# Attention's products placed on tiles of the TensorE array: two heads on two partition halves

## The chip, the cores and the metric

One core of one Trainium2 chip runs the whole program in one launch. The metric is the device time of an execution in microseconds (us). TensorE is called PE here, VectorE DVE, ScalarE ACT, GpSimd POOL, and SyncE, which issues most DMAs, SP. PEld is PE's loading of weights, which the profile lists apart from its matmuls.

## The reference

A linear attention with a decaying state (batch B = 4, heads H = 8, sequence S = 768, head dimension D = 48) is followed by a mixture of experts with one expert per token (N = 3072 tokens, width 384, E = 8 experts, inner width F = 1024). All arrays are 32-bit floats.

```
for t in range(S):                       # attention, per batch and head
    cur = einsum('bhd,bhe->bhde', u * k_t, v_t)
    y_t = einsum('bhd,bhde->bhe', r_t, state + cur)
    state = w * state + einsum('bhd,bhe->bhde', k_t, v_t)
x = y as (N, 384)
e_idx = argmax(x @ w_gate, axis=1)       # top-1 routing
gate_w = softmax(x @ w_gate)[token, e_idx]
eom = sigmoid(x @ w_output_gate)
out[token] = gate_w * eom[token, e] * (relu(x @ w1[e]) @ w2[e])   # e = e_idx
```

## The kernel before, in words

Attention is done in chunks of C = 128 tokens: 6 chunks per batch, 24 in all. Inside a chunk r and k are multiplied by powers of w (tables `PR` and `PK`), so that the decay between two tokens becomes a product. The loop `for i in range(NT)` in `rwkv_top1_moe` walks the chunks, and for each it walks the list `STEP` (`STEP0` for chunk 0), in which each short name is a piece of work handed out by `act`. The whole stretch is in manual order: each engine runs its instructions as the program writes them.

The pieces of a chunk, by their names in `STEP`:

- `s0`, `s1` (`scores`): q = 0..3 is a pair of heads, j the head in the pair. A transposed K of a pair has 96 partitions (2 x 48). `KT` holds it twice, each copy with the other head's rows set to zero (a scale by `k.block`), so a 96-row matmul gives one head's 128 x 128 scores. DVE multiplies them by the causal mask into `A[j]` (L281).
- `st` (`state`): K^T V for a pair, 96 x 96 with two unwanted off-diagonal blocks, which the decay `WT` sets to zero. DVE adds the old state (L302), POOL multiplies by `WT` (L303).
- `in` (`inter`): r times the old state, 4 matmuls into the bank `ps_y`.
- `i0`, `i1` (`intra`): masked scores times v, 8 matmuls into the same bank.
- `tr` (`trans`): the next chunk's K and R are transposed on PE (L266) and copied by ACT, K twice (L271), R once (L268).
- `xt`, `lm`, `lt`: the finished chunk's output x is transposed (L363), copied by ACT, multiplied by the router's two weights into 16 logits (L370), which ACT copies out a chunk later.
- `p0`, `p1` (`prep`, L213), `ut` (`uterm`, POOL) and `bo` (`bonus`): r and k times the powers, and the term with u. `ld` loads chunk i + 3. After the list, `output` adds the u-term to `ps_y` (L325) and stores x.
- `m` (`micro`), `t1`, `t5`: small steps of the router's grouping program, some on DVE, some on PE.

All these matmuls are in 32-bit floats; the profile shows each as two records of a weight load and a matmul, and each transpose as one. The experts behind attention use fp32r matmuls, with one record each. The first expert's first rows are gathered and multiplied while the last chunk and the last router group are finished.

Of the kernel before, what the change touches and what calls it, by code (L numbers as in the profile page):

```python
# [41 lines left out]
HW = 2 * D  # L42
# [5 lines left out]
STEP = ['lt', 's0', 'm', 's1', 'm', 'xt', 'ld', 'ut', 'bo', 'm', 'p0', 'm', 'p1', 'st', 'm', 'in', 'tr', 't5', 'm', 'i0', 'i1', 'lm', 't1']  # L48
# [83 lines left out]
def make_flag(tc, pool, pspool, k):  # L132
    nc = tc.nc
    ok = pool.tile([HW, NP], F32, name="ok")
# [3 lines left out]
    nc.tensor.matmul(ps[:, :NP], k.ones[:HW], ok, start=True, stop=True)  # L138
    return ps


def read_flag(tc, pool, ps, k):
# [4 lines left out]
    nc.vector.tensor_scalar(k.flag, low, float(HW) - 0.5, None, op0=ALU.is_ge)  # L147


def make_powers(tc, pool, k, halfway):  # L150
    nc = tc.nc
    M = C // 2
    sq = [pool.tile([HW, NP], F32, name=f"sq{i}") for i in range(8)]
    pr = pool.tile([HW, NP, C], F32, name="pr_t")
# [1238 lines left out]
```

## Time and profile before

| | us |
|---|---|
| median of 3 runs | 433.81 (431.82 to 435.5) |
| profiled execution | 432.96 |
| its span | 431.2 |
| first scores of chunk 0 | start at 8.23 |
| scores of chunk 23, the last | start at 170.85 |
| PE busy | 405.2 (94%) |
| DVE busy | 259.4 (60%) |
| ACT busy | 170.5 (40%) |
| POOL busy | 175.7 (41%) |

The profiled execution took 1.76 us more than its span, from the first to the last instruction. A page of the profile counts an engine as busy from an instruction's start to its end; PE's ends are modelled, and neighbouring matmuls overlap, so a block's price on PE is read from start to start. Bracketed times in an order of time are the idle time before an instruction, with what ended it. In the groups, the columns are busy time, mean nanoseconds of one, and idle time ahead with its releasers. The granted clock of PE is 0.979 of full speed as a mean over the span, and 1.00 in attention from 0 to 160 us.

### The profile page before, as it was taken

What the parts mean: (1) busy time and instruction counts of PE and PEld (TensorE: products, weight loads), DVE (VectorE), ACT (ScalarE), POOL (GpSimd) and SP (SyncE); (2) the same over time, 40 slices, a digit from 0 to 9 for tenths busy, and PEclk for the clock granted to TensorE, in tenths of its full rate; (3) what the DMA queues carried; (4) which work ended last, traced back from release to release, by engine and by line L of the source; (5) the groups of instructions that cost most, each with busy time, mean ns of one, the idle gap of its engine ahead of it and who ended that gap; (6) DMA issues with size and microseconds to landing.
All of it is one profiled execution on the core that took longest, in us unless ns stands there. A gap on an engine that the chain in (4) does not pass through costs nothing. (4 is left out here: it accounts for less than half of the span.)

```text
span 431.2 us, 8139 instructions
## 1 busy us (share of the span) xinstructions
PE 405.2 (94%) x2948; PEld 396.6 (92%) x2948; DVE 259.4 (60%) x592; ACT 170.5 (40%) x339; POOL 175.7 (41%) x210
## 2 busy tenths in 40 slices
PE   7899999999999989995998999999999999999980
PEld 5899999999999989995997999999999999999980
DVE  6966698597769996381676356166274653636300
ACT  4323333342425344421545255265363552535210
POOL 6965446646456779523115031132212502301020
PEclk9999999999999999898899999999999999999996
DMA  7855646464557753006427336365274472840010
GB/s 138 175 114 109 136 87 147 95 129 109 111 112 181 204 137 121 21 19 218 138 85 245 111 117 198 96 194 169 58 241 148 132 233 75 258 127 34 2 42 20
DMA packets 104669, 54.83 MB, mean 127 GB/s; under 512 B 78495, under 2 KB 102227, under 8 KB 104608
## 3 DMA queue, kind: packets, MB, share of 16 engines
q1 hardware_dynamic: 101184, 44.27, 39.7%
q0 software_dynamic: 3424, 9.82, 6.9%
q8 instruction: 29, 0.48, 0.5%
q14 instruction: 32, 0.26, 0.2%
HBM read 44.64 MB, written 9.76 MB: 126 GB/s over the span
## 5 line engine op out<-in xcount | busy, mean ns | idle before, releaser
L835 POOL DMA_INDIRECT out_dram<-yo,si x28 | 28.5, 1018 | 135.5 <-ACT yo L832 72.8
L798 PE MATMUL ps_h<-xh,w1h 128*128 128x384 f32 (+4 forms) x216 | 74.0, 343 | 6.5 <-issue 4.7
L799 PE MATMUL ps_h<-xl,w1h 128*128 128x384 f32 (+4 forms) x216 | 72.2, 334 | 0.0
L800 PE MATMUL ps_h<-xh,w1l 128*128 128x384 f32 (+4 forms) x216 | 72.1, 334 | 0.0
L769 POOL DMA_INDIRECT xg<-x_d,gi x28 | 31.5, 1125 | 44.6 <-PE ps_xt L781 29.8
L798 PEld LDWEIGHTS ps_h<-xh,w1h 128*128 128x128 f32 x216 | 42.3, 196 | 7.6 <-issue 5.0
L279 PE MATMUL ps_a<-RT,KT 96*128 96x128 f32 x384 | 48.6, 280 | 0.4 <-DVE RT L231 0.4
L808 DVE SCALAR_TENSOR_TENSOR hl<-ps_h,hh 128x384 fp32r<-128x384 f32 (+4 forms) x72 | 37.8, 532 | 17.4 <-ACT hh L807 17.1
L807 ACT ACTIVATE hh<-ps_h 128x384 fp32r<-128x384 f32 (+4 forms) x72 | 33.6, 472 | 33.0 <-PE ps_h L800 33.0
L279 PEld LDWEIGHTS ps_a<-RT,KT 96*128 96x128 f32 x384 | 44.8, 192 | 0.8 <-DVE RT L231 0.8
L860 PE MATMUL ps_o<-w2h,hh 128*128 128x384 f32 x128 | 43.5, 340 | 0.0
L861 PE MATMUL ps_o<-w2l,hh 128*128 128x384 f32 x128 | 42.9, 335 | 0.0
L862 PE MATMUL ps_o<-w2h,hl 128*128 128x384 f32 x128 | 42.8, 335 | 0.0
L281 DVE TENSOR_TENSOR A<-ps_a,mask 128x512 f32<-128x512 f32 x48 | 32.6, 684 | 16.6 <-PE ps_a L279 16.5
L800 PEld LDWEIGHTS ps_h<-xh,w1l 128*128 128x128 f32 x216 | 42.3, 196 | 0.2
L799 PEld LDWEIGHTS ps_h<-xl,w1h 128*128 128x128 f32 x216 | 42.3, 196 | 0.1
L747 DVE TENSOR_TENSOR w1l<-raw,w1h 128x768 fp32r<-128x768 f32 x28 | 26.7, 954 | 23.4 <-ACT w1h L746 23.4
L271 ACT ACTIVATE KT<-ps_t,block 96x512 f32<-96x512 f32 x46 | 28.9, 678 | 27.9 <-PE ps_t L266 27.9
L319 PE MATMUL ps_y<-v_t,A 128*128 128x48 f32 x336 | 39.7, 271 | 0.0
L319 PEld LDWEIGHTS ps_y<-v_t,A 128*128 128x128 f32 x336 | 39.2, 192 | 0.0
L746 ACT CAST w1h<-raw 128x768 fp32r<-128x768 f32 (+1 forms) x36 | 27.2, 764 | 27.0 <-PE ps_h L799 17.4
L253 POOL TENSOR_TENSOR vc<-v_t,coef 128x384 f32<-128x384 f32 x21 | 21.9, 1044 | 38.0 <-DVE coef L251 27.5
(222 smaller groups left out, 808.6 us busy)
## 6 DMA issues: line engine op xcount, KB each, us to landing
raw<-in_moe_w_dram SPq DMA_DIRECT2D x64, 384.0 KB, 4.9
x_d<-x SPq DMA_DIRECT2D x24, 192.0 KB, 2.0
k_t<-in_k_dram SPq DMA_DIRECT2D x21, 192.0 KB
r_t<-in_r_dram SPq DMA_DIRECT2D x21, 192.0 KB, 4.8
v_t<-in_v_dram SPq DMA_DIRECT2D x21, 192.0 KB, 4.7
raw<-in_k_dram SPq DMA_DIRECT2D x3, 192.0 KB
raw<-in_r_dram SPq DMA_DIRECT2D x3, 192.0 KB
xg<-x_d,gi POOLq DMA_INDIRECT x28, 4.8
```

The lines of the kernel that those rows point to most:

```text
L279: nc.tensor.matmul(pa[:, q, :], KT[:, q, j, :], RT[:, q, :], start=True, stop=True)
L281: nc.vector.tensor_mul(a, pa, k.mask.unsqueeze(1).to_broadcast((C, NP, C)))
L319: nc.tensor.matmul(self.y[:, D * h : D * (h + 1)], A[j][:, h // 2, :], vt[:, h, :], start=(i % NCH == 0 and h == 0), stop=(h == H - 1), sk ...
L769: nc.gpsimd.indirect_dma_start(out=self.xg[q][:n], out_offset=None, in_=self.x_d[:n_x, :], in_offset=bass.IndirectOffsetOnAxis(ap=self.rt. ...
L798: nc.tensor.matmul(o, wh[:, j, fs], xh, start=(j == 0), stop=False)
L799: nc.tensor.matmul(o, wh[:, j, fs], xl, start=False, stop=False)
L800: nc.tensor.matmul(o, wl[:, j, fs], xh, start=False, stop=(j == KC - 1))
L807: nc.scalar.activation(hh, o, AF.Relu)
L808: nc.vector.scalar_tensor_tensor(hl, o, 0.0, hh, op0=ALU.max, op1=ALU.subtract)
L860: nc.tensor.matmul(o, hh, wh, start=(f == 0), stop=False)
L861: nc.tensor.matmul(o, hh, wl, start=False, stop=False)
L862: nc.tensor.matmul(o, hl, wh, start=False, stop=(f == FC - 1))
```

## The change: what it does

Head j of a pair now lives on partitions 64 j to 64 j + 47, with zeros in the 16 partitions above. `Rn` and `Kn` become fixed tiles with 64 columns per head, whose last 16 columns are set to zero once. The tables, the powers and the state follow that layout, and `k.block`, `WT` and K's second copy are gone. Each product is then written for a part of the array:

- scores: for each head 48 rows (its half of the partitions) and, in two column halves c, 64 of the 128 keys: 16 matmuls in place of 8, in tiles of 64 x 64. The two heads' products are interleaved, and the two masks (`a0`, `a1`) follow the whole block (`sc`).
- inter: the same quarters, 16 matmuls in place of 4. `ps_y` has two banks, one for each head j.
- intra, state and logits: all 128 rows, 64 columns: 16, 8 and 6 matmuls in place of 8, 4 and 3, in tiles of 128 x 64.

The state is 128 x 192 in place of 96 x 384, without the off-diagonal blocks. `xt` takes its PSUM bank from the two score banks (`at`), and the logits take theirs from the state's (`u`); logits are multiplied and copied out in one step, `lm`, a chunk earlier. `STEP` is written in another order, the loading of w comes in two DMAs behind a memset on DVE, and k and r of chunk 0 are loaded into tiles padded in the same way.

PE in one chunk before (chunk 3; `ps_a` are scores, `ps_x` transposes of the output and then logits, `ps_u` the state, `ps_y` inter and intra, `ps_t` transposes of the next chunk):

```order
L279 MATMUL ps_a_576<-RT,KT 128x128 x4
L279 MATMUL ps_a_583<-RT,KT 128x128 x4
L363 MATMUL ps_x<-ident,x 128x128 x3
L295 MATMUL ps_u<-v_t,Kn 96x96 x4
L312 MATMUL ps_y<-T,RT 128x96 x4
L266 MATMUL ps_t<-ident,Kn 96x128 x4
L266 MATMUL ps_t<-ident,Rn 96x128 x4
L319 MATMUL ps_y<-v_t,A_581 128x48 x4
L319 MATMUL ps_y<-v_t,A_588 128x48 x4
L370 MATMUL ps_x<-wg_149,xT 128x16 x3
```

PE in one chunk after (chunk 4; only the last two of eight rows of scores are shown, and `ps_l` are the logits):

```order
L277 MATMUL ps_a_771<-RT,KT 64x128 x2
L277 MATMUL ps_a_772<-RT,KT 64x128 x2
L315 MATMUL ps_y<-T,RT 64x48 x16
L372 MATMUL ps_x<-ident,x 128x128 x3
L264 MATMUL ps_t<-ident,Kn_301 128x128 x4
L264 MATMUL ps_t<-ident,Rn_298 128x128 x4
L382 MATMUL ps_l<-wg_151,xT 64x16 x6
L323 MATMUL ps_y<-v_t,A_789 64x48 x8
L293 MATMUL ps_u<-v_t,Kn_300 64x48 x8
L323 MATMUL ps_y<-v_t,A_791 64x48 x8
```

Inter has moved up behind the scores, the state from in front of the transposes to between the two halves of intra, and the logits from the end to in front of intra. Scores and inter stand side by side, and so do all products in column halves.

DVE in one chunk without router steps before (masks, u-term's sum, R and K times their powers, the state's add, the output):

```order
L281 TENSOR_TENSOR A_1209<-ps_a_1204,mask 128x512
L281 TENSOR_TENSOR A_1216<-ps_a_1211,mask 128x512
L251 TENSOR_REDUCE coef<-ku 128x8
L213 TENSOR_TENSOR Rn<-r_t,PR 128x384
L213 TENSOR_TENSOR Kn<-k_t,PK 128x384
L302 TENSOR_TENSOR T_1247<-ps_u,T 96x384
L325 TENSOR_TENSOR x<-ps_y,vc 128x384
```

DVE in such a chunk after:

```order
L281 TENSOR_TENSOR A_1404<-ps_a_1386,mask 128x512
L281 TENSOR_TENSOR A_1406<-ps_a_1387,mask 128x512
L249 TENSOR_REDUCE coef<-ku 128x8
L217 TENSOR_TENSOR Rn_298<-r_t,PR 128x8x48
L217 TENSOR_TENSOR Kn_301<-k_t,PK 128x8x48
L301 TENSOR_TENSOR T_1486<-ps_u,T 128x192
L330 TENSOR_TENSOR x<-ps_y,vc 128x384
```

The order on DVE is the same; the state's add has half the columns, and R and K are written with a step of 64 per head.

The diff, cut to its core:

```
-STEP = ['lt', 's0', 'm', 's1', 'm', 'xt', 'ld', 'ut', 'bo', 'm', 'p0', 'm', 'p1', 'st', 'm', 'in', 'tr', 't5', 'm', 'i0', 'i1', 'lm', 't1']
+STEP = ['m', 'sc', 'a0', 'm', 'a1', 'in', 'xt', 't1', 'm', 'tr', 't1', 'ld', 'ut', 'bo', 'm', 'p0', 'm', 'p1', 'lm', 'i0', 'st', 'i1', 'm']
...
-    k.wt = pool.tile([HW, NP], F32, name="wt")
-    tc.nc.sync.dma_start(k.wt, w.rearrange("(q j) d -> (j d) q", j=2))
+    k.wt = pool.tile([C, NP], F32, name="wt")
+    tc.nc.vector.memset(k.wt, 1.0)
+    for j in range(2):
+        tc.nc.sync.dma_start(k.wt[HB * j : HB * j + D], w.rearrange("(q j) d -> j d q", j=2)[j])
...
+        self.Rn, self.Kn = ([self.pw.tile([C, H, HB], F32, name=f"{nm}{i}", bufs=1) for i in range(n)] for nm, n in (("Rn", 2), ("Kn", 3)))
+        for t in self.Rn + self.Kn:
+            tc.nc.gpsimd.memset(t[:, :, D:], 0.0)
...
-            if src is Rn:
-                nc.scalar.copy(RT, p[:HW])
-            else:
-                for j in range(2):
-                    nc.scalar.activation(KT[:, :, j, :], p[:HW], AF.Copy, scale=k.block[:, j, 0:1])
+            nc.scalar.copy(dst, p)
...
-        pa = ps.tile([C, NP, C], F32, name=f"ps_a{j}", tag="at", bufs=2)
+        self.pa = [ps.tile([C, NP, C], F32, name=f"ps_a{j}", tag="at", bufs=2) for j in range(2)]
         for q in range(NP):
-            nc.tensor.matmul(pa[:, q, :], KT[:, q, j, :], RT[:, q, :], start=True, stop=True)
+            for j in range(2):
+                rows = slice(HB * j, HB * j + D)
+                for c in range(2):
+                    half = slice(HB * c, HB * (c + 1))
+                    nc.tensor.matmul(self.pa[j][half, q, :], KT[rows, q, half], RT[rows, q, :], start=True, stop=True)
...
-        for q in range(NP):
-            nc.tensor.matmul(U[:HW, HW * q : HW * (q + 1)], Kf[:, HW * q : HW * (q + 1)], vt[:, 2 * q : 2 * q + 2, :], start=True, stop=True)
+        for h in range(H):
+            j, q = h % 2, h // 2
+            nc.tensor.matmul(U[HB * j : HB * (j + 1), D * q : D * (q + 1)], Kn[:, h, :], vt[:, h, :], start=True, stop=True)
...
-                nc.tensor.matmul(self.y[:, HW * q : HW * (q + 1)], RT[:, q, :], self.T[:, q, :], start=(q == 0), stop=False, skip_group_check=True)
+                for j in range(2):
+                    rows = slice(HB * j, HB * j + D)
+                    for c in range(2):
+                        half = slice(HB * c, HB * (c + 1))
+                        nc.tensor.matmul(self.y[half, j, D * q : D * (q + 1)], RT[rows, q, half], self.T[rows, q, :], start=(q == 0), stop=False, skip_group_check=True)
...
-        for h in range(j, H, 2):
-            nc.tensor.matmul(self.y[:, D * h : D * (h + 1)], A[j][:, h // 2, :], vt[:, h, :], start=(i % NCH == 0 and h == 0), stop=(h == H - 1), skip_group_check=True)
+        for q in range(NP):
+            for c in range(2):
+                half = slice(HB * c, HB * (c + 1))
+                nc.tensor.matmul(self.y[half, j, D * q : D * (q + 1)], A[j][:, q, half], vt[:, 2 * q + j, :], start=(i % NCH == 0 and q == 0), stop=(q == NP - 1), skip_group_check=True)
...
-        px = ps.tile([C, 512], F32, name="ps_x", tag=tag, bufs=1)
+        px = ps.tile([C, 512], F32, name="ps_x", tag=tag, bufs=bufs)
...
+        pl = ps.tile([C, 512], F32, name="ps_l", tag=tag, bufs=1)
         for j in range(KC):
-            self.tc.nc.tensor.matmul(px[:, DM : DM + 2 * E], xT[:, j, :], self.wg32[:, j, :], start=(j == 0), stop=(j == KC - 1), skip_group_check=True)
+            for c in range(2):
+                half = slice(HB * c, HB * (c + 1))
+                self.tc.nc.tensor.matmul(pl[half, : 2 * E], xT[:, j, half], self.wg32[:, j, :], start=(j == 0), stop=(j == KC - 1), skip_group_check=True)
...
-                                X[i - 1] = rt.logits_t(ps, rw, x)
+                                X[i - 1] = rt.logits_t(ps, rw, x, "at", 2)
```

More of the change, by code (lines that the diff above doesn't have):

```diff
@@ L41 @@
 EARLY = 2
-HW = 2 * D
+HB = 64
 ORDER_AT = 14
@@ L137, in make_flag @@
     ps = pspool.tile([C, 512], F32, name="ps_flag", tag="g", bufs=1)
-    nc.tensor.matmul(ps[:, :NP], k.ones[:HW], ok, start=True, stop=True)
+    nc.tensor.matmul(ps[:, :NP], k.ones, ok, start=True, stop=True)
     return ps
@@ L152, in make_powers @@
     M = C // 2
-    sq = [pool.tile([HW, NP], F32, name=f"sq{i}") for i in range(8)]
-    pr = pool.tile([HW, NP, C], F32, name="pr_t")
-    pk = pool.tile([HW, NP, C], F32, name="pk_t")
+    sq = [pool.tile([C, NP], F32, name=f"sq{i}") for i in range(8)]
+    pr = pool.tile([C, NP, C], F32, name="pr_t")
+    pk = pool.tile([C, NP, C], F32, name="pk_t")
     nc.vector.memset(pr[:, :, M : M + 1], 1.0)
@@ L178, in make_tables, with load_rkv @@
     for src, dst in ((k.pk, k.PK), (k.pr, k.PR)):
-        ps = pspool.tile([C, NP, HW], F32, name="ps_pw", tag="tr", bufs=2)
+        ps = pspool.tile([C, H, HB], F32, name="ps_pw", tag="tr", bufs=2)
         for q in range(NP):
-            nc.tensor.transpose(ps[:, q, :], src[:, q, :], k.ident[:HW, :HW])
-        nc.scalar.copy(dst.rearrange("p h d -> p (h d)"), ps.rearrange("p q d -> p (q d)"))
-    for q in range(NP):
-        nc.scalar.activation(k.WT[:, q, :], k.block.rearrange("p j d -> p (j d)"), AF.Copy, scale=k.w128[:, q : q + 1])
-def load_rkv(tc, pin, spare, srcs, b, c, after=None):
+            nc.tensor.transpose(ps[:, 2 * q : 2 * q + 2, :], src[:, q, :], k.ident)
+        nc.scalar.copy(dst, ps[:, :, :D])
+def load_rkv(tc, pin, spare, srcs, b, c, first, after=None):
     nc = tc.nc
@@ L217, in first @@
         nc, k = self.tc.nc, self.k
-        RT = self.pw.tile([HW, NP, C], F32, name="RT")
-        KT = self.pw.tile([HW, NP, 2, C], F32, name="KT")
         ts = self.load(0)
-        p = [None, None]
+        RK = [None, None]
         for n in (1, 0):
-            p[n] = ps.tile([C, NP, C], F32, name="ps_f", tag="at", bufs=2)
+            p = ps.tile([C, NP, C], F32, name="ps_f", tag="at", bufs=2)
             warm_up(self.tc, k, WARM[2 + n])
             for q in range(NP):
-                nc.tensor.transpose(p[n][:HW, q, :], ts[n][:, 2 * q : 2 * q + 2, :], k.ident)
-        pk = [self.pw.tile([HW, NP, C], F32, name=f"pk{j}", tag=f"A{j}") for j in range(2)]
-        for j in range(2):
-            nc.scalar.activation(pk[j], k.pk, AF.Copy, scale=k.block[:, j, 0:1])
-        nc.vector.tensor_mul(KT[:, :, 0, :], p[1][:HW], pk[0])
-        nc.vector.tensor_mul(RT, p[0][:HW], k.pr)
-        nc.vector.tensor_mul(KT[:, :, 1, :], p[1][:HW], pk[1])
-        self.st[0] = [None, None, ts[2], RT, KT]
+                nc.tensor.transpose(p[:, q, :], k.raw0["rk"[n]][:, 2 * q : 2 * q + 2, :], k.ident)
+            RK[n] = self.pw.tile([C, NP, C], F32, name=("RT", "KT")[n])
+            nc.vector.tensor_mul(RK[n], p, (k.pr, k.pk)[n])
+        self.st[0] = [None, None, ts[2]] + RK
     def uterm(self, i):
@@ L1150, in load @@
             if i < NT and i not in ready:
-                ready[i] = load_rkv(tc, pin and pin[0], spare, (r, kk, v), *divmod(i, NCH), after)
+                ready[i] = load_rkv(tc, pin and pin[0], spare, (r, kk, v), *divmod(i, NCH), k.raw0 if i == 0 else {}, after)
             return ready.get(i)
+        k.raw0 = {}
+        for nm in "kr":
+            k.raw0[nm] = const.tile([C, H, HB], F32, name=f"{nm}0")
+            nc.gpsimd.memset(k.raw0[nm][:, :, D:], 0.0)
         load(0)
```

115 lines of the change are left out of this document (56 added, 59 removed).

## The prediction

> **What bounds the kernel now.** I read the page's header first, then the busy time of the engines in stages of 20 us, then the order in time on TensorE (PE) for one chunk, then the groups of instructions.
>
> ```profile
> span 431.2 us, 8139 instructions
> PE 405.2 (94%) x2948; PEld 396.6 (92%) x2948; DVE 259.4 (60%) x592; ACT 170.5 (40%) x339; POOL 175.7 (41%) x210
> ```
>
> ```profile
> core 0: us, PE busy (x) PEld busy (x) DVE busy (x) ACT busy (x) POOL busy (x), PEclk, DMA share, GB/s
> 20.00:40.00 20.00, 20.00 (x188) 20.00 (x186) 12.60 (x21) 6.92 (x15) 12.43 (x14) 1.00 0.58 125
> 40.00:60.00 20.00, 20.00 (x190) 20.00 (x189) 15.16 (x41) 7.38 (x17) 10.11 (x10) 1.00 0.51 111
> 60.00:80.00 20.00, 20.00 (x190) 20.00 (x189) 15.76 (x37) 7.16 (x16) 12.08 (x13) 1.00 0.56 119
> 80.00:100.00 20.00, 19.25 (x181) 19.09 (x180) 17.51 (x47) 7.63 (x18) 11.75 (x11) 1.00 0.48 102
> 100.00:120.00 20.00, 20.00 (x190) 20.00 (x189) 14.28 (x39) 7.27 (x16) 11.62 (x11) 1.00 0.55 119
> 120.00:140.00 20.00, 19.33 (x183) 19.17 (x182) 17.16 (x50) 8.29 (x18) 11.31 (x12) 1.00 0.67 157
> 140.00:160.00 20.00, 18.36 (x174) 18.01 (x174) 19.20 (x55) 7.64 (x19) 14.58 (x16) 1.00 0.64 170
> ```
>
> In attention PE is never idle, while VectorE (DVE) works 111.67 of these 140 us. Only the last stage turns round: DVE is at 19.20 and PE waits a little. So PE sets the pace, with DVE 20% behind.
>
> The chunk's order in time on PE (start, length with the pipeline's tail, and a count of records; a 32-bit matmul leaves two records, a transpose one):
>
> ```profile
> 22.40 2.03 PE L279 MATMUL ps_a<-RT,KT 96*128 96x128 f32 x16
> ...
> 62.38 0.81 PE L370 MATMUL ps_x<-wg,xT 128*128 128x16 f32 x6
> 63.04 2.03 PE L279 MATMUL ps_a<-RT,KT 96*128 96x128 f32 x16
> 64.90 0.49 PE L363 MATMUL ps_x<-ident,x 128*128 128x128 f32 x3
> 65.23 0.84 PE L295 MATMUL ps_u<-v_t,Kn 128*96 128x96 f32 x8
> 65.91 1.06 PE L312 MATMUL ps_y<-T,RT 96*128 96x96 f32 x8
> 66.81 0.60 PE L266 MATMUL ps_t<-ident,Kn 128*96 128x128 f32 x4
> 67.24 0.60 PE L266 MATMUL ps_t<-ident,Rn 128*96 128x128 f32 x4
> 67.68 1.88 PE L319 MATMUL ps_y<-v_t,A 128*128 128x48 f32 x16
> 69.40 0.81 PE L370 MATMUL ps_x<-wg,xT 128*128 128x16 f32 x6
> ...
> 170.85 2.03 PE L279 MATMUL ps_a<-RT,KT 96*128 96x128 f32 x16
> ```
>
> Start to start gives each block's price: scores 1.86, output transposes 0.33, state 0.68, inter 0.90, input transposes 0.87, intra 1.72, logits 0.66: 7.02 us. The scores of chunk 2 start at 22.40 and those of chunk 23 at 170.85, so a chunk takes 148.45 / 21 = 7.07 us: the PE blocks back to back. The 32-bit products are 5.82 of it.
>
> What sets a record's pace is the weight load. Intra streams only 48 columns yet takes 1.72 / 16 = 0.107 us a record; with 96 instead of 128 weight columns the state takes 0.68 / 8 = 0.085. For 64 columns that makes 0.054 (half of 0.107) to 0.063 (the line through both). The stream's price shows where the load is short:
>
> ```profile
> 319.00 0.49 PE L845 MATMUL ps_o<-ident,yt 128*128 128x128 f32 x3
> ...
> 319.50 0.33 PE L799 MATMUL ps_h<-xl,w1h 128*128 128x384 f32 x1
> ...
> 324.72 0.49 PE L845 MATMUL ps_o<-ident,yt 128*16 128x128 f32 x3
> ...
> 325.23 0.34 PE L799 MATMUL ps_h<-xl,w1h 128*128 128x384 f32 x1
> ```
>
> With 16 weight columns three transposes are no quicker than with 128. So 128 streamed columns cost the 0.109 us of an input transpose (0.87 / 8), 48 cost 0.041.
>
> **TensorE's products.** The change doubles or quadruples their number: scores 8 to 16 matmuls, inter 4 to 16, intra 8 to 16, state 4 to 8, logits 3 to 6, so 54 records a chunk become 124, each with 64 weight columns. All hangs on how far records of different array tiles overlap, and no row of before shows two tiles at work. From both sides:
> - No overlap: scores 32 x 0.109, the other 92 records x 0.054: 3.49 + 4.97 = 8.46 us, against 5.82.
> - Full overlap (four tiles in scores and inter, two in the rest): 3.49 / 4 + 32 x 0.054 / 4 + 60 x 0.054 / 2 = 0.87 + 0.43 + 1.62 = 2.92 us.
> [...]
>
> [...]
>
> ```profile
> 90.71 0.18 PE L461 MATMUL ps_c<-oh,tri 128*128 128x40 bf16 x1
> ...
> 90.86 1.36 PE L279 MATMUL ps_a<-RT,KT 96*128 96x128 f32 x10
> ```
>
> Six loads and six matmuls pass between 90.71 and 90.86 (two lines with five of them are left out), 0.025 us a pair, so 124 pairs need 3.1 us: issuing does not stand in the way of any gain. [...]
>
> [...]
>
> I take 3.7, just above the middle of 2.92 and 4.23, because the four products of a pair of heads read different rows or write different columns and nothing in their operands orders them, while d is not quite nothing.
>
> The way into row tiles has a row. [...]
>
> ```profile
> 249.26 0.44 PEld L781 LDWEIGHTS ps_xt<-ident,xg 128*128 128x128 f32 x3
> 249.87 0.48 PEld L781 LDWEIGHTS ps_xt<-ident,xg 24*128 24x128 f32 x4 [0.17 <-issue]
> ```
>
> The load engine stands 0.17 us at each such entry; column tiles (the 16-column rows above, 0.51 against 0.50 us) cost nothing. Scores and inter stand together, so there is one stay per chunk: 0.17. [...] Transposes keep 0.33 + 0.87 (128 instead of 96 weight columns stay below the stream's 0.109). PE per chunk: 3.7 + 1.2 + 0.17 = 5.1 us, 4.3 to 7.2 over overlap and order.
>
> **What is late next: DVE.**
>
> ```profile
> L281 DVE TENSOR_TENSOR A<-ps_a,mask 128x512 f32<-128x512 f32 x48 | 32.6, 684 | 16.6 <-PE ps_a L279 16.5
> L302 DVE TENSOR_TENSOR T<-ps_u,T 96x384 f32<-96x384 f32 x16 | 8.7, 543 | 0.0
> L303 POOL TENSOR_TENSOR T<-T,WT 96x384 f32<-96x384 f32 x16 | 16.1, 1004 | 14.7 <-DVE T L302 14.4 <-DVE parts L447 0.3
> L325 DVE TENSOR_TENSOR x<-ps_y,vc 128x384 f32<-128x384 f32 x24 | 13.3, 553 | 15.8 <-PE ps_y L319 12.1 <-issue 1.4 <-POOL ku L241 1.1
> L271 ACT ACTIVATE KT<-ps_t,block 96x512 f32<-96x512 f32 x46 | 28.9, 678 | 27.9 <-PE ps_t L266 27.9
> L268 ACT COPY RT<-ps_t 96x512 f32<-96x512 f32 x23 | 13.2, 573 | 0.0
> ```
>
> Before, DVE waits 16.5 + 12.1 us for scores and outputs; a quicker PE takes these waits away, but not its work. The state's add falls from 384 to 192 columns; by the masks (512 columns, 0.684) and the add (384, 0.543) a column costs 0.0011 us, so it saves 0.21. The strided output (reading two banks) and the padded prep keep their element counts: between -0.05 and +0.1 us a chunk, 0 taken. DVE per chunk: 111.67 / 140 x 7.07 = 5.64 - 0.21 = 5.43 us.
>
> Stage by stage (2.83 chunks each) the larger of DVE - 0.6 and PE at 5.1 x 2.83 = 14.4: 14.4, 14.6, 15.2, 16.9, 14.4, 16.6, 18.6: 110.7 us. Even in its fullest stage DVE reached 19.20 / 20 = 0.96, so 110.7 / 0.96 = 115.3 where 140 stood: 24.7 us less. Chunk 23 and the stretch behind it move forward unchanged.
>
> **Edits that hide or nearly so.** ScalarE (ACT) makes one K copy at RT's 0.573 where two of 0.678 stood, 0.78 us less, on an engine with 12 of 20 us free: worth nothing by itself. GpSimd's (POOL) decay works on half the columns, 0.5 to 1.0 us, and `in` waits for it; the scores stand ahead of `in` and cover it. New waits on PE: the output transposes now take the score buffers, so they wait for the first mask (0.684 behind the scores) with `tr` and all products queued behind; `in` (0.4 to 0.9) covers all but 0 to 0.3. The state takes the logits' bank and waits for their ACT copy, which stands behind the K and R copies; behind it waits `i1`. From the end of the K transposes ACT needs 2 x 0.573, PE 0.44 + 0.3 to 0.6 + 0.4 to 0.9 to get there: 0 to 0.3 late. Both fit into PE's slack to DVE (5.43 / 0.96 - 5.1 = 0.55); without that slack they would cost up to 0.6 x 22 = 13 us. At the start
>
> ```profile
> 0.97 0.48 DVE L85 MEMSET warm<- 128x512 bf16 x1 [0.97 <-PEq L1380]
> ...
> 8.09 0.68 DVE L232 TENSOR_TENSOR KT<-ps_f,pk 96x512 f32<-96x512 f32 x1
> ```
>
> the third DVE product falls away (0.68 less ahead of the second half of the first scores), but the decays' load waits for a memset that is at most as long as the 0.48 of a larger one: -0.7 to +0.5, 0 taken. Seven POOL memsets stand ahead of work that waits for loads anyway.
>
> **The sum.** The profiled execution took 432.96 (span 431.2 and 1.76 around it; the median of the runs is 433.81, 0.2% more). 432.96 - 24.7 = 408.3, and I round the strided accesses against it: 409 us.
>
> **Rivals.** (1) Loads go one at a time: tiles stream side by side but there is one way for weights. 124 x 0.054 = 6.70 us, PE at 6.70 + 1.2 + 0.17 = 8.07, 1.05 more than its blocks now; 24 chunks: +25, so 458 us. It decides as soon as less than a sixth of the load time overlaps: at today's 7.02 us the products may take 7.02 - 1.37 = 5.65 of those 6.70. For it: loads, not streams, set today's pace, and PEld is busy all through; against it: each half's loads go to other rows or columns. With 0.063 a load: 485. Chance 0.15. (2) Tiles do not overlap at all, so the change doesn't do what it says: 8.46 + 1.37 - 7.02 = +2.8 a chunk, 500 us; 0.05. [...] (4) Full overlap with DVE smooth across stages: 5.43 x 21 / 0.96 = 119 instead of 148 us, 403; in my range.
>
> **Chances.** Forecast and (4) together 0.63, a middling 420 to 428 us 0.05, (3) 0.12, (1) and (2) 0.20. About 1% can be told from no change here, so faster 0.68, same 0.12, slower 0.20. The forecast's own range is 400 to 420 (PE 4.3 to 5.9 a chunk, waits 0 to 0.3); with (3) and the near edge of (1) 400 to 440, leaving out 0.2, nearly all of it above.
>
> **What would show it.** Right: chunks about 5.8 us apart, 32-bit blocks summing to 3 to 4.5 us, DVE over 90% busy from 20 us on with few waits for the scores, a gap of about 0.2 us ahead of the scores' loads. Rival (1): PEld busy throughout, scores taking 1.7 us or more and intra unchanged at 1.7. [...] Wrong altogether: PE idle at the output transposes, the state or `in`, with chunks of 7 us.

## The result, and the profile after

The kernel after takes 422.06 us (median of 4 runs, 421.79 to 422.51), the kernel before beside it 433.0 us: a ratio of 0.974, with a 95% interval of 0.969 to 0.979. It is 10.9 us faster, where the forecast of 409 us had it 24.0 us faster; 422.06 us lies 13.1 us above the forecast, although inside its range. The profiled execution took 422.51 us, its span 420.8.

The page's header and the busy time by stages of 20 us of the kernel after:

```profile
span 420.8 us, 11171 instructions
...
PE 372.9 (89%) x4500; PEld 352.2 (84%) x4500; DVE 256.6 (61%) x592; ACT 152.1 (36%) x310; POOL 165.5 (39%) x215
```

```profile
core 0: us, PE busy (x) PEld busy (x) DVE busy (x) ACT busy (x) POOL busy (x), PEclk, DMA share, GB/s
20.00:40.00 20.00, 18.98 (x530) 17.43 (x529) 15.13 (x26) 5.36 (x14) 13.67 (x17) 0.96 0.67 145
40.00:60.00 20.00, 15.67 (x362) 14.11 (x362) 18.31 (x50) 5.53 (x15) 10.68 (x12) 0.91 0.57 123
...
100.00:120.00 20.00, 16.06 (x438) 14.30 (x432) 18.93 (x56) 5.51 (x15) 12.46 (x15) 1.00 0.68 152
120.00:140.00 20.00, 16.32 (x340) 14.90 (x342) 16.44 (x50) 7.74 (x20) 12.11 (x13) 0.83 0.78 196
140.00:160.00 20.00, 17.07 (x360) 15.59 (x356) 15.73 (x44) 5.61 (x14) 11.28 (x13) 0.74 0.26 76
```

The roles have turned round as forecast: PE now has idle time in every stage, and from 40 to 140 us DVE is the fuller engine in the stages shown. But the column behind POOL's, the granted clock, was 1.00 in all of these stages before. Now it goes down to 0.74, and in the last two stages neither engine is full.

A chunk without router steps, in order of time on PE:

```profile
63.92 1.10 PE L277 MATMUL ps_a<-RT,KT 48*64 48x128 f32 x32
64.85 0.63 PE L315 MATMUL ps_y<-T,RT 48*64 48x48 f32 x32
65.81 0.55 PE L372 MATMUL ps_x<-ident,x 128*128 128x128 f32 x3 [0.33 <-DVE A L281]
66.19 0.60 PE L264 MATMUL ps_t<-ident,Kn 128*128 128x128 f32 x4
66.63 0.60 PE L264 MATMUL ps_t<-ident,Rn 128*128 128x128 f32 x4
67.16 0.53 PE L382 MATMUL ps_l<-wg,xT 128*64 128x16 f32 x12
67.53 0.65 PE L323 MATMUL ps_y<-v_t,A 128*64 128x48 f32 x16
68.03 0.67 PE L293 MATMUL ps_u<-v_t,Kn 128*64 128x48 f32 x16
68.53 0.64 PE L323 MATMUL ps_y<-v_t,A 128*64 128x48 f32 x16
69.10 0.45 PE L277 MATMUL ps_a<-RT,KT 48*64 48x128 f32 x8
```

Start to start: scores 0.93 (1.86 before), inter 0.63 (0.90), logits 0.37 (0.66), intra 0.50 + 0.57 (1.72), state 0.50 (0.68). The 32-bit products take 3.50 us, entry into the row tiles included, where 5.82 stood, and the chunk 5.18 instead of 7.02. PE is idle in it for the 0.33 us that it waits for the mask and for nothing else, and DVE works 4.23 us, so a chunk like this still goes at PE's pace. If all 21 chunks from 22 us on were like this one, some 40 us would be gone (148.45 - 21 x 5.18). Four chunks that lost much of it follow (windows from one chunk's scores to the next; the first is the quiet chunk above, chunk 9, the others are 13, 18, 21 and 22, with router steps):

```profile
63.92:69.10 5.18, 4.85 (x139) 4.50 (x135) 4.23 (x8) 1.53 (x4) 3.54 (x4) 1.00 0.68 148
85.63:94.12 8.49, 6.51 (x139) 5.83 (x135) 6.98 (x17) 2.06 (x5) 4.39 (x4) 0.80 0.44 95
116.30:126.69 10.39, 7.02 (x108) 6.36 (x104) 8.15 (x21) 3.04 (x7) 6.14 (x7) 0.70 0.90 223
140.42:150.78 10.36, 7.69 (x139) 6.93 (x135) 8.81 (x18) 3.04 (x7) 6.53 (x8) 0.69 0.28 79
150.78:157.71 6.93, 6.93 (x142) 6.53 (x140) 4.25 (x16) 2.45 (x6) 3.02 (x4) 0.72 0.28 87
```

Each of these four is longer than its DVE work by 1.5 to 2.7 us, and has a clock of 0.69 to 0.80. The three things that PE waited for most from 22 to 180 us (total, times, longest):

```profile
PE ps_x L372 <- DVE A L281: 13.2, 17, 3.4
PE ps_y L315 <- DVE x L330: 5.1, 5, 2.0
PE ps_xt L793 <- DMA xg<-x_d,gi: 3.0, 1, 3.0
```

The longest of these, in chunk 18, begins on DVE, whose order has router steps between a chunk's products and the next masks:

```profile
117.90 0.89 DVE L520 TENSOR_TENSOR ohp<-pp,ip 128x512 bf16<-128x512 f32 x1
118.71 0.95 DVE L459 CAST parts<-rest 128x4 bf16<-128x4 f32 x1
119.58 0.54 DVE L330 TENSOR_TENSOR x<-ps_y,vc 128x384 f32<-128x384 f32 x1
120.04 0.68 DVE L281 TENSOR_TENSOR A<-ps_a,mask 128x512 f32<-128x512 f32 x1
```

PE waits 3.37 us for that mask, and from 120.5 us its clock is halved (0.50 for 6.8 us). Before, PE was late enough for DVE's router steps to fit in nearly unseen: from 22 to 180 us it waited three times for DVE, 1.5 us at the longest.

Where the span's 10.4 us came from: the scores of chunk 2 start 0.2 us later (22.63), the 21 chunks up to the scores of chunk 23 take 135.08 instead of 148.45 us (-13.4), and the rest 263.1 instead of 260.4 (+2.7). Forecast were 0, -24.7 and 0.

### The profile page after: what moved, and what is told of

It is laid out like the page before. It is cut to its first block, busy times and chain, and to the rows that moved or that the text cites. A ratio compares the mean times of both kernels' runs of the same rounds, so it can differ in the third digit from the quotient of the medians.

```text
span 420.8 us, 11171 instructions
## 1 busy us (share of the span) xinstructions
PE 372.9 (89%) x4500; PEld 352.2 (84%) x4500; DVE 256.6 (61%) x592; ACT 152.1 (36%) x310; POOL 165.5 (39%) x215
## 5 line engine op out<-in xcount | busy, mean ns | idle before, releaser
L374 ACT COPY xT<-ps_x 128x384 f32<-128x384 f32 x24 | 11.5, 479 | 91.7 <-PE ps_x L372 83.6
L759 DVE TENSOR_TENSOR w1l<-raw,w1h 128x768 fp32r<-128x768 f32 x28 | 26.7, 955 | 23.4 <-ACT w1h L758 21.0
L281 DVE TENSOR_TENSOR A<-ps_a,mask 128x512 f32<-128x512 f32 x48 | 31.3, 683 | 5.7 <-PE ps_a L277 5.7
L796 DVE TENSOR_TENSOR xl<-ps_xt,xh 128x384 fp32r<-128x384 f32 (+4 forms) x27 | 13.9, 538 | 32.4 <-ACT xh L795 32.1
L251 POOL TENSOR_TENSOR vc<-v_t,coef 128x384 f32<-128x384 f32 x21 | 21.3, 1014 | 28.0 <-DVE coef L249 18.1
L759 DVE TENSOR_TENSOR w2l<-raw,w2h 128x768 fp32r<-128x768 f32 x28 | 26.7, 958 | 7.4 <-ACT w2h L758 5.7
L758 ACT CAST w2h<-raw 128x768 fp32r<-128x768 f32 (+1 forms) x36 | 26.7, 765 | 8.4 <-PE ps_o L874 4.4
L323 PE MATMUL ps_y<-v_t,A 128*64 128x48 f32 x672 | 29.3, 237 | 0.0
```

Of the source, the lines that this page charges most:

```text
L281: self.tc.nc.vector.tensor_mul(a, self.pa[j], self.k.mask.unsqueeze(1).to_broadcast((C, NP, C)))
L758: nc.scalar.copy(hi, self.raw[i][:, cs])
L759: (eng or nc.vector).tensor_sub(lo, self.raw[i][:, cs], hi)
```

## The experiments

Two theories stood against each other. Theory 1: what is missing is the clock; a gap in PE's work halves it, the halved PE is late with the next scores and states, DVE waits for them, and the next chunk starts late too. Theory 2: what is missing is DVE's; its router steps bunch in single chunks and stop PE there, and the low clock only accompanies that. A third, that the tiles overlap less than forecast, is answered by the 3.50 us above as far as the size goes, but not as to why; same_tile below is for that.

**fill: the gaps filled, nothing else moved.**

```
+FILL = {(6, 'wx'): 7, (7, 'wy'): 4, (8, 'wx'): 3, (13, 'wy'): 8, (18, 'wx'): 14, (20, 'wy'): 7, (21, 'wy'): 6, (21, 'wx'): 6}
-STEP = ['m', 'sc', 'a0', 'm', 'a1', 'in', 'xt', ...
+STEP = ['m', 'sc', 'a0', 'm', 'a1', 'wy', 'in', 'wx', 'xt', ...
+    for _ in range(n):       # 'wy', 'wx': n fillers into the next K transposition's bank
+        nc.tensor.matmul(self.pt..., self.k.warm[:, :C], self.k.warm, start=True, stop=True)
```

> The changed kernel with 55 extra BF16 matmuls of 512 columns (about 0.21 us each at full clock; their results go into the bank of the next K transposition and are overwritten) put in front of the eight places where TensorE waits longest between chunks 6 and 21 (16 and 39 of them ahead of the inter-chunk products and of the x transposes). Nothing else moves. Theory 1 (the idle gaps of TensorE pull its granted clock down, and the halved clock lengthens the chunks): the granted clock of chunks 6, 13, 18, 21 and 22 goes from 0.69-0.80 to 0.95 or more, these chunks come down to their VectorE time plus about 0.6 us (6: 7.9 to 7.0, 13: 8.5 to 7.3, 18: 10.4 to 8.6, 21: 10.4 to 9.3, 22: 6.9 to 5.3), 6 to 8 us in all: 414 to 416 us. Theory 2 (VectorE's order alone sets these chunks, and the clock only follows): clock up, but time within 2 us of the changed kernel, 420 to 424 us.

Measured: 414.19 us (411.48 to 419.8), 0.954 of before. Chunks 13, 18, 21 and 22 have a clock of 1.00 and take 7.30, 7.78, 7.75 and 5.89 us. Chunk 7, which had a clock of 1.00 in the kernel after, now had 0.83 and took 9.84: its four fillers left waits of 1.6 and 0.7 us. Nearly all is as theory 1 had it.

**masks_first: DVE's order mended instead.**

```
-STEP = ['m', 'sc', 'a0', 'm', 'a1', 'in', ... 'i0', 'st', 'i1', 'm']
+STEP = ['sc', 'a0', 'a1', 'm', 'm', 'm', 'in', ... 'i0', 'st', 'i1']
```

> The changed kernel with the three router slots at the chunk's two ends moved behind both masks, so that VectorE does the output addition and the two masks of a chunk without router steps between them. Theory 1: TensorE's waits ahead of the x transposes and of the inter-chunk products (13.2 and 5.1 us between 22 and 180 us) fall to under 8 us together, so the clock stays above 0.9 in most chunks: 6 to 9 us gained, 413 to 416 us. Theory 2 (VectorE is the bound in router chunks whatever the order): waits move from the masks to T1 and to the next chunk's loads, and the time stays within 3 us of 422. Both have the quiet chunks at 5.2 us.

Measured: 421.41 us (417.78 to 425.54); the profiled run is the fastest of these. In it PE's waits for masks and outputs fell from 18.3 to 13.1 us only, while new ones of 3.6 us came up (for the state's decay on POOL and a router product), and chunks 1, 2, 18 and 20 had clocks of 0.80, 0.58, 0.66 and 0.75. This fits theory 2's number, but does not separate the two: the order did not take the gaps away, it moved them.

**same_tile: the same products in another order.** Four in a row go to one tile.

```
-for q in range(NP):          # scores, inter
-    for j in range(2):
-        for c in range(2):
+for j in range(2):
+    for c in range(2):
+        for q in range(NP):   # and c outside q in intra, j outside q in state
```

> The changed kernel with the quarter and half products in another order: the four head pairs (q) run innermost, so that four products in a row go to the same array tile and the tiles change only every fourth. Theory A (products overlap because neighbours sit in different tiles, as the forecast's sum of 3.7 us supposed): scores go from 0.9 to about 2 us, the f32 products of a chunk from 3.2 to 5 us or more, quiet chunks from 5.2 to 6.5 us and more, 445 us and up. Theory B (it is the smaller tile itself that is cheap, not the alternation): blocks within 0.1 us of those of the changed kernel, 420 to 424 us.

Measured: 440.28 us (438.5 to 445.92), 1.014 of before (1.005 to 1.023). A quiet chunk, with the scores and the start of inter in it:

```profile
80.71:87.76 7.05, 7.05 (x137) 6.77 (x136) 4.34 (x8) 1.53 (x4) 3.53 (x4) 1.00 0.53 115
```

```profile
80.71 2.24 PE L277 MATMUL ps_a<-RT,KT 48*64 48x128 f32 x29
82.68 0.31 PE L315 MATMUL ps_y<-T,RT 48*64 48x48 f32 x2
```

PE is full again, and the quiet chunk as long as before (7.05 and 7.02 us). From their start to that of inter the scores take 1.97 us, 0.062 for each of their 32 records (three of them come behind the first of inter, so the row counts 29); in the kernel after it is 0.93 / 32 = 0.029. The starts of the single records show why. In both kernels they form chains in which one record follows another by 0.109 us. In the kernel after four such chains run side by side, with starts 0.007 us apart. In same_tile a new chain begins 0.49 us behind the last one, and only two run at a time. Theory A is right: the gain comes from neighbours in different tiles. A smaller tile alone gave nothing here.

**gap: gaps put into quiet chunks.**

```
+GAPS = {2: 1, 4: 3, 9: 5}
+    for _ in range(GAPS.get(i, 0)):     # ahead of the first mask
+        nc.vector.tensor_mul(junk[:, 0], junk[:, 1], k.mask.unsqueeze(1).to_broadcast((C, NP, C)))
```

> The changed kernel with extra VectorE products of 128x512 (about 0.65 us each, on a tile that nobody reads) ahead of the first mask in three quiet chunks: 1 in chunk 2, 3 in chunk 4, 5 in chunk 9, so that TensorE waits ahead of the x transposes 0.65, 2.0 and 3.3 us longer than the 0.33 us it waits there now. Theory 1 (a gap halves the clock): chunk 2 keeps clock 1.00, chunk 9 and perhaps chunk 4 fall to 0.7-0.8 and grow by 1 us and more beyond the VectorE time added. Theory 2: the granted clock stays 1.00 in all three, and each chunk grows by the VectorE time added less the 0.5 to 0.9 us that VectorE waits there now (chunk 2 by under 0.3, chunk 4 by 1.1 to 1.5, chunk 9 by 2.4 to 2.8 us).

Measured: 443.39 us in one run, 21 more than the kernel after, for 9.3 us of added DVE work. Chunks 3, 4, 5, 9 and 10:

```profile
30.07:35.24 5.17, 4.84 (x139) 4.50 (x135) 4.23 (x8) 1.53 (x4) 3.54 (x4) 1.00 0.68 148
35.24:45.89 10.65, 7.47 (x140) 6.93 (x136) 7.55 (x11) 1.82 (x4) 4.60 (x5) 0.67 0.38 79
45.89:53.21 7.32, 7.32 (x122) 6.82 (x120) 4.77 (x8) 1.82 (x4) 5.57 (x6) 0.55 0.51 110
77.75:89.85 12.10, 7.47 (x139) 6.92 (x135) 8.94 (x13) 1.82 (x4) 4.59 (x5) 0.73 0.31 67
89.85:97.83 7.98, 7.98 (x138) 7.48 (x136) 4.15 (x8) 1.82 (x4) 3.31 (x4) 0.56 0.47 102
```

Chunks 4 and 5 took 17.97 us together instead of 9.84 in the kernel after (5.18 and 4.66): 8.1 us lost, with 3.3 us more DVE work in chunk 4. Chunks 9 and 10 lost 9.7 for 4.7. PE waited 3.2 and 4.6 us (the added products took 1.03 us each in the mean instead of the 0.65 expected). With the added work as it was, theory 2 would have chunk 4 grow by 2.4 to 2.8 and chunk 9 by 3.8 to 4.2 us. So these two gaps cost 2.5 and 2.1 times their 3.2 and 4.6 us. Chunk 2 says nothing: its clock was already 0.59, because PE had waited 2.55 us for DVE's output in chunk 1.

**gap_small: how long a gap must be.** GAPS = {3: 1, 9: 2, 16: 3}, otherwise as gap.

> The changed kernel with extra VectorE products of 128x512 ahead of the first mask: 1 in chunk 3, 2 in chunk 9, 3 in chunk 16, to find the length of a TensorE wait from which the clock halves: waits of about 1.0, 1.7 and 2.3 us. Theory 1, by the waits seen so far (1.1 us left the clock alone, 1.7 us and more mostly did not): chunk 3 at 1.00 and within 0.3 us of 5.2, chunk 9 on the edge, chunk 16 at 0.8 or less with a slow chunk 17. Theory 2: the clock 1.00 throughout.

Measured: 426.72 us in one run. Waits of 0.5, 1.8 and 3.3 us gave clocks of 1.00, 0.79 and 0.65, and chunks of 5.59, 8.15 and 11.03 us. But the waits of the router chunks speak against a plain threshold: one of 1.6 us (chunk 6) and one of 1.8 (chunk 18) left the clock at 1.00, one of 1.7 (chunk 20) brought 0.81. The reason shows in windows of 3.41 us of the kernel after, set so that the halvings fall on their edges:

```profile
41.99:45.40 3.41, 1.94 (x64) 1.64 (x60) 3.34 (x7) 0.47 (x3) 2.30 (x3) 1.00 0.66 142
45.40:48.81 3.41, 3.20 (x26) 3.12 (x28) 2.30 (x10) 1.62 (x3) 1.44 (x2) 0.51 0.92 186
48.81:52.22 3.41, 2.91 (x86) 2.48 (x84) 3.41 (x16) 0.29 (x3) 1.34 (x2) 0.99 0.02 5
...
117.08:120.49 3.41, 0.32 (x12) 0.08 (x4) 3.41 (x9) 0.40 (x1) 2.83 (x3) 1.00 0.95 256
120.49:123.90 3.41, 3.13 (x23) 2.80 (x23) 3.41 (x10) 1.54 (x3) 1.23 (x2) 0.51 0.82 189
```

Here the windows with 1.94 and 0.32 us of PE work are each followed by one at a clock of 0.51. In the trace of the kernel after all 17 changes of the clock, from 7.9 to 414.1 us, lie whole multiples of 3.413 us apart. With one grid of 3.413 us laid from 12 to 190 us over the kernel after, gap and gap_small each, all 19 windows at full clock with at most 1.94 us of PE work were followed by a halved one, and none with 1.99 or more. So among these waits of 1.6 to 1.8 us it is where they fall in the window that decided. In masks_first and fill single windows with 1.78 and 1.88 us stayed at full clock, and so did one of the kernel before with 1.94, its emptiest from 12 to 170 us, and one of fill_all with 1.54, behind attention; the edge is not sharp. The halved stretches of the kernel after from 12 to 190 us are one to three windows long (3.4, 6.8 and 10.2 us), one of whole_intra is four (13.7), and a wait of 1.7 us (chunk 6 of the kernel after) was enough to bring one.

**fill_all: fillers at all the places.** Those of fill, with 10 in chunk 7, 8 in chunk 1, a few in 12, 19 and 22, and 12 ahead of the transposes (L793) that wait for the gathered rows.

```
+FILL: (7, 'wy'): 10, (1, 'wy'): 8, (12, 'wx'): 3, (19, 'wy'): 2, (22, 'wy'): 2
+    if tail:                  # chunk 23, ahead of ex.early_x(ps)
+        for _ in range(12):
+            nc.tensor.matmul(hot, k.warm[:, :C], k.warm, start=True, stop=True)
```

> The kernel with fillers, with more of them: 8 ahead of the inter-chunk products of chunk 1, 10 instead of 4 in chunk 7 (which the first fillers left at a clock of 0.83 with 2.3 us of waits), 2 or 3 in chunks 12, 19 and 22, and 12 ahead of the transposes that wait for the gathered rows in chunk 23. Theory 1 (idle gaps halve the clock): chunk 7 comes down from 9.8 to 7.3 us, no chunk under a clock of 0.95, and the stretch from the last scores to the first l2 product loses 1 to 2 us: 408 to 412 us. Theory 2 (what is left is VectorE's work): 413 to 416 us as with the first fillers.

Measured: 410.49 us (408.88 to 411.33), 0.946 of before (0.943 to 0.950). Chunks 6, 13, 18, 21 and 22, the last four of which stand with their longer times in the result above:

```profile
41.34:47.41 6.07, 6.07 (x120) 4.80 (x116) 5.97 (x18) 1.96 (x6) 3.63 (x4) 1.00 0.79 167
...
83.12:90.42 7.30, 6.98 (x147) 5.21 (x143) 6.98 (x17) 1.84 (x5) 4.40 (x4) 1.00 0.41 89
112.59:120.38 7.79, 7.53 (x122) 5.23 (x118) 7.79 (x20) 2.75 (x7) 4.96 (x6) 1.00 0.92 232
134.13:141.89 7.76, 7.75 (x151) 5.53 (x148) 7.72 (x17) 2.75 (x7) 5.99 (x7) 1.00 0.34 97
141.89:147.79 5.90, 5.89 (x147) 4.94 (x143) 5.08 (x18) 2.45 (x6) 3.59 (x5) 1.00 0.30 97
```

From chunk 1 to the scores of chunk 23 the clock is 1.00 in every chunk, and the five chunks shown are 0.0 to 0.8 us longer than their DVE work. The 88 fillers are about 19 us of more work for PE (12 of them take 2.59 us), and the kernel is 11.6 us faster for it. That is theory 1's size: 8.4 us are gained in the chunks from 2 on, 1.5 at the start and 1.3 behind chunk 23. The gain lies where the clock was low: the six chunks from 2 on that had less than 1.00 in the kernel after (6, 13, 18, 19, 21, 22) take 40.6 us instead of 49.8, the other fifteen 86.0 instead of 85.3. One chunk speaks a little for theory 2: chunk 7 takes 8.67 us against 7.24, since its DVE work grew from 6.73 to 8.16 us. Chunk 6 gave 1.80 us back, so the two together gained 0.4.

**fill_late: the gathered rows later.**

```
-    ex.early_x(ps)            # in 'xt' of chunk 23, behind 12 fillers
+    ex.early_x(ps)            # behind 'i1', behind 8 fillers
```

> As fill_all, but in chunk 23 the transposes of the gathered rows stand behind the intra products instead of ahead of them, with 8 fillers in front. If the wait for the gather is a loss of its own and not only the trigger of a low clock, the 1 us of intra products now runs inside it: 0.7 to 1.3 us under fill_all. If the router's last steps on VectorE set the stretch, no difference.

Measured: 412.11 us (410.65 to 414.02), 1.6 over fill_all instead of under it. PE still waited 1.7 us for the gather and then 1.1 for DVE, and the clock of the 20 us from chunk 23's scores on was 0.83, 1.00 in fill_all. The intra products did not run inside the wait to any gain; since the clock was low here, the run does not show what their place alone is worth.

**masks_fill: the other order with fillers.** The STEP of masks_first with FILL = {(1, 'wy'): 10, (6, 'wx'): 4, (7, 'wy'): 10, (12, 'wx'): 5, (18, 'wx'): 9, (20, 'wx'): 13, (21, 'wx'): 5, (22, 'wy'): 3}, and chunk 23's 12.

> masks_first with fillers at its own waits (chunks 1, 6, 7, 12, 18, 20, 21, 22 and the gather of chunk 23). Theory 1 (the order of VectorE's steps mattered only through the clock): with the clock near 1.00 the two orders give the same time, 408 to 413 us. If the stalls of TensorE behind the router's steps are a cost of their own: 404 to 407 us.

Measured: 414.9 us (411.03 to 415.54). One stall was missed (3.5 us in chunk 19, with a clock of 0.70 and 11.50 us for that chunk). It points to the order of DVE's steps being worth nothing by itself, since even without that stall it would only come near fill_all, but it is not a clean test.

**before_gap and before_gap2: is it the tiles that bring the low clock?** The kernel before, with added DVE products ahead of the first mask of chunks 4 and 9: first 3 and 5, then 8 and 11.

```
+GAPS = {4: 3, 9: 5}           # before_gap2: {4: 8, 9: 11}
+    for _ in range(GAPS.get(i, 0)):     # 's0', ahead of scores and mask
+        nc.vector.tensor_mul(junk[:, 0], junk[:, 0], k.mask.unsqueeze(1).to_broadcast((C, NP, C)))
```

> The kernel before, unchanged but for 3 extra VectorE products of 128x512 ahead of the first mask of chunk 4 and 5 ahead of that of chunk 9 (about 2.0 and 3.3 us). Theory 1 (any gap of TensorE of that length halves the clock, and the kernel before was spared only because TensorE never ran dry): the granted clock of chunks 4 or 5 and of 9 and 10 falls to 0.8 or less, and those four chunks take 6 us or more longer than now, 438 us and up. Theory 3 (the halved clock belongs to the quarter and half tiles): the clock stays at 1.00 and the chunks grow only by the VectorE time beyond its slack, under 4 us together, 433 to 437 us.

> The kernel before with 8 extra VectorE products ahead of the first mask of chunk 4 and 11 ahead of that of chunk 9 (about 5.3 and 7.3 us), enough to use up VectorE's slack and leave TensorE waiting 2.5 us or more. Theory 1: the clock falls to 0.5 in the next 3.4 us and more, in a kernel without array tiles too; chunks 4, 5, 9 and 10 take 12 us or more longer than the 28.0 us of now. Theory 3 (only quarter and half tiles bring the halving): clock 1.00, and these chunks grow by the work added less its slack, 6 to 9 us.

Measured: 436.76 and 458.51 us, one run each. The first missed: DVE's slack swallowed the products, PE waited 0 and 0.8 us, so neither theory was tried in chunks 4 and 9. But in its chunk 1, which has no added products, PE waited 2.3 us for DVE (0.9 in the kernel before); the clock was 0.85 there and the chunk took 11.1 us instead of 8.1. The second made waits of 2.4 and 5.5 us. Chunks 4, 5 and 6 of it:

```profile
36.89:48.84 11.95, 9.53 (x68) 9.27 (x67) 10.59 (x16) 2.38 (x5) 4.27 (x5) 0.80 0.31 67
48.84:60.94 12.10, 12.10 (x58) 12.03 (x59) 3.97 (x6) 2.38 (x5) 4.68 (x5) 0.50 0.31 65
60.94:70.50 9.56, 9.56 (x63) 9.50 (x64) 6.56 (x16) 2.52 (x6) 3.30 (x3) 0.64 0.39 82
```

In the kernel before they take 7.02, 6.32 and 6.25 us. With a wait of 2.4 us among them they take 14 us longer, and the clock stayed halved for 24. So it is not the tiles: the kernel before was spared because PE had no gap of that length (1.5 us at the longest).

**whole_fill and whole_intra: the column halves of intra and logits undone,** in fill_all and in the kernel after.

```
-for c in range(2):
-    half = slice(HB * c, HB * (c + 1))
-    nc.tensor.matmul(self.y[half, j, ...], A[j][:, q, half], vt[:, 2 * q + j, :], ...)
+nc.tensor.matmul(self.y[:, j, ...], A[j][:, q, :], vt[:, 2 * q + j, :], ...)
```

> The kernel fill_all with the column halves undone: intra products and logits in full width of 128 columns again (16 instead of 32 and 3 instead of 6 products of that kind counted by heads), scores, inter-chunk products and state as changed. All chunks are at a clock of about 1.00 in both, so the difference is the price of the halves alone. Theory A (TensorE and VectorE are near balance in quiet chunks, 4.85 to 5.1 us of 5.18): intra and logits grow by about 0.7 and 0.3 us, quiet chunks become TensorE-bound at 5.8 to 6.1 us, router chunks hardly change: 6 to 10 us over fill_all, 416 to 420 us. Theory B (VectorE alone sets the pace and the halves were not needed): under 2.5 us over fill_all, 411 to 413 us.

> The changed kernel with the column halves of intra products and logits undone (full width of 128 columns), scores, inter-chunk products and state as changed, no fillers. It is run because whole_fill, which showed quiet chunks at 6.37 us (against 5.18), also showed 42 us at a halved clock with TensorE at work all the time, so that its total prices nothing. Theory A: quiet chunks are again at 6.3 to 6.4 us, router chunks about as in the changed kernel, 436 to 442 us. If that long halved stretch comes from the fillers together with a TensorE that never rests, it is absent here; if it comes from the full-width products among tiles, it is here too and the time is 445 us or more.

Measured: whole_fill ran between 433.12 and 452.63 us, so that its total is not used; whole_intra took 448.73 us (448.19 to 451.82), 1.035 of before. Their quiet chunks agree: 6.37 us, 1.19 more than with halves, which is what these two column tilings are worth where PE sets the pace. In chunks 2 to 13 of whole_fill, all at a clock of 1.00 as in fill_all, undoing them cost 11.0 us (80.3 and 69.3), more than theory A had for the whole kernel. In the ten chunks from 2 on that have a clock of 1.00 in both whole_intra and the kernel after, it is 10.1 us (62.8 and 52.7). At these rates the halves are some 19 to 21 of whole_intra's 26.7 us over the kernel after, an estimate, and the rest is clock. The long halved stretch is in whole_intra too, so the fillers did not make it. Chunks 9, 10, 11, 21 and 22 of whole_intra:

```profile
75.39:81.76 6.37, 6.04 (x114) 5.75 (x113) 4.23 (x7) 1.58 (x4) 3.54 (x5) 1.00 0.57 127
81.76:88.13 6.37, 6.04 (x114) 5.76 (x113) 4.67 (x9) 1.58 (x4) 3.54 (x5) 1.00 0.60 128
88.13:94.95 6.82, 6.82 (x99) 6.67 (x98) 5.17 (x13) 1.90 (x5) 4.66 (x6) 0.75 0.55 118
161.24:172.94 11.70, 11.11 (x115) 10.68 (x114) 7.75 (x14) 2.64 (x6) 7.47 (x9) 0.50 0.15 50
172.94:184.64 11.70, 11.70 (x120) 11.25 (x119) 4.97 (x19) 2.64 (x6) 2.87 (x5) 0.50 0.17 52
```

The clock falls in chunk 11, although PE waited no more than 0.3 us at a time in the chunks ahead of it, and from 160 us on it stays halved for 41 us, with PE at work for all but 0.6 us of chunks 21 and 22. What the clock goes by is then not the busy time of the records alone. One count from the traces comes nearer: the streamed columns of the records that start in a window, each record's times the share of 128 x 128 that its rows and weight columns fill. In all runs but same_tile, from 12 us to the scores of chunk 23, the 25 windows at full clock with at most 1456 were all followed by a halved one, and none of the 436 with more than 1584; of the 14 between, 5 were. But in same_tile 16 windows with 912 to 1448 kept the full clock. So what it counts was not found out.

## Why the prediction was right and wrong

**Right in the main: what bounds the kernel, and what replaces it.** PE set the pace, and in the chunks with router steps DVE does where the clock allows it; in the quiet ones PE still does. The stretch from the scores of chunk 2 to those of chunk 23, in the kernel after and in fill_all:

```profile
22.63:157.71 135.08, 113.54 (x2737) 103.18 (x2733) 116.82 (x302) 40.85 (x106) 79.95 (x88) 0.91 0.61 140
```

```profile
21.15:147.79 126.64, 119.11 (x2806) 99.33 (x2802) 117.11 (x302) 39.86 (x106) 80.85 (x89) 1.00 0.66 150
```

DVE works 116.82 / 21 = 5.56 us a chunk; 5.43 were forecast. The state's add fell from 0.543 to 0.354 us, about as forecast, but all of DVE's work in these chunks only from 118.57 to 116.82 us. The 5.56 us are a mean over 4.23 us in quiet chunks, under PE's 4.85, and up to 8.81 in chunks with router steps.

**Right, with a better size: the tiles.** The 32-bit products were taken at 3.7 + 0.17 us and measured 3.50 with all entries. No run shows the 4.23 us and the d that the 3.7 leans on, nor the 7.2 us at the far end of PE's range: in their place the quiet chunk has 3.50 us for these products and 4.85 of PE's work in all. In its scores a record follows the one ahead of it in its tile by 0.109 us, while those of the other tiles start 0.007 us apart, and the block took 0.93 us. So rival (3), with its chance of 0.12, is out. The reason given in the forecast held in same_tile: with four neighbours in one tile a record takes 0.062 us, against 0.029. The 0.17 us for entering the row tiles, read ahead of loads of 24 rows, did not come: ahead of the scores' loads (L277) the load engine stands 1.3 us in all from 22 to 158 us, 0.06 a chunk. Rivals (1) and (2) needed 6.70 and 8.46 us. PEld is busy 4.50 of 5.18 us in the quiet chunk, so busy time alone would not have ruled out rival (1).

**Wrong: "In attention PE is never idle", carried over with its clock.** PE was idle for 0.7 to 1.6 us in three of the seven stages shown there, but never for more than 1.5 us at a time. The step that failed is the one that took every PE price, and the stages' sums, at a clock of 1.00 after PE had become the engine that waits. The stages' maximum then hid where the waits lie: in the stage from 40 to 60 us DVE is busy 18.31 and PE 15.67 us, which looks like 4.3 us of harmless idle time, but 1.68 us of it stand in one piece, and behind it the clock is halved (0.51 from 45.40 to 48.81 us). With the clock kept at 1.00 (fill_all) the same chunks take 126.64 us from the scores of chunk 2 to those of chunk 23, against a forecast of 148.45 - 24.7 = 123.75, and the kernel 410.49 us against 409. So for a kernel at full clock the sum was good to 2.9 us in these chunks. That the whole comes nearer owes something to luck: chunk 23 and what follows took 1.4 us more than before, and the start 1.25 us less. By fill_all the clock is 11.6 of the 13.1 us by which the forecast missed.

**Wrong: 0.96 as DVE's share.** It is 116.82 / 135.08 = 0.86 in these chunks. With the clock at 1.00 it is 117.11 / 126.64 = 0.92. Of the missing 0.10, 0.06 are the clock; the rest are DVE's waits for scores and states (3.3 and 2.7 us in fill_all), which no fullest stage of before could show.

**Wrong: "Chunk 23 and the stretch behind it move forward unchanged."** They took 2.7 us more. The gather that was in time before is late:

```profile
163.21 1.83 PE L793 MATMUL ps_xt<-ident,xg 128*128 128x128 f32 x6 [2.97 <-DMA xg<-x_d,gi]
```

POOL issues this gather when the router's last step on DVE is done:

```profile
158.78 1.23 POOL L781 DMA_INDIRECT xg<-x_d,gi  x1 [0.40 <-DVE sc L610]
```

That is 1.1 us behind the start of chunk 23's scores (157.71); before, the issue at 166.38 was 4.5 us ahead of them (170.85). The 21 chunks took 13.4 us less, DVE's work in them 1.75 us less, and the halved clock follows here too. With fillers 1.4 us of the 2.7 remain.

**The start** was put at 0 and came to +0.2 at the scores of chunk 2. The priced new waits, for ACT's copy of the logits and for the score banks, are there with 0.2 to 0.6 and 0.33 us. The score banks' wait was to fit into PE's slack to DVE. In quiet chunks there is no such slack: PE's 4.85 us and the wait's 0.33 are the whole 5.18, so it is paid. In router chunks the same wait is the one that grows to 3.4 us.

## What to carry to other kernels

When a change takes the lead from TensorE, look at how its new idle time is spread, not only at how much there is: waits of 2.4 to 5.5 us that were put in cost about two to six times their length, because the clock was halved for the next 3.4 us or several times that (24 us in before_gap2). Where the waits were not taken away, matmuls on data that is there anyway, put just ahead of the waiting instruction, kept the clock at 1.00 from chunk 1 to the scores of chunk 23 here: 88 of them made this kernel 11.6 us faster. In this kernel products on array tiles gained only where neighbours in the order go to different tiles (0.029 us a record of the scores, against 0.062 in same_tile).

## What the runs showed of the hardware

- The clock's changes lie on a grid of 3.413 us (all 17 in the kernel after, all 5 in the kernel before). A window at full clock with at most 1.94 us of TensorE work was followed by half clock, one with 1.99 or more was not (19 windows in the kernel after, gap and gap_small), with a few at 1.54 to 1.94 on the other side in other runs (1.54 in fill_all, 1.78 in masks_first, 1.88 in fill, 1.94 in the kernel before).
- Recovery differs: one to three windows in the kernel after (3.4 to 10.2 us), four in whole_intra (13.7), 24 us in before_gap2 after a wait of 2.4 us, 41 us in whole_intra behind no wait of over 0.6 us. A window with 3.41 us of work among full-width products of 48 columns was followed by half clock too (85.01 to 88.42 us of whole_intra, ahead of chunk 11, then 0.50).
- 32-bit records of 64 weight columns come every 0.029 us in four alternating tiles (scores of the kernel after, 128 streamed columns), every 0.062 where four products in a row go to one tile (same_tile), and every 0.031 in two alternating tiles (intra of the kernel after, 48 streamed columns, 0.50 / 16). The records of one chain of scores follow each other by 0.109 us, and chains in different tiles start 0.007 us apart.
- The added DVE products of 128x512 on data in SBUF took 1.03 us in the mean in gap, masks of that size, which read PSUM, 0.68. In the kernel after K times its powers (128x384, in SBUF) took 0.52 us at 51.03 us with POOL idle and 1.19 at 25.90 us, where POOL's product with v (L251) ran beside it for 65% of that time.
